# Attention by groups of heads: value products in five stretches of a unit instead of seven

## The chip, the core and the metric

The kernel runs on one core of one Trainium2 chip. The metric is the device time of one execution in microseconds; the time of a kernel is the median of its runs. Engines are called by the names of the profile: PE is TensorE (its matrix products), PEld its weight loads, ACT is ScalarE, DVE is VectorE, POOL is GpSimd, SP is SyncE, which issues most transfers.

## The reference

One layer over 2048 tokens of width 448, in float32: a gate mixes an attention branch A and a token-mixing and MLP branch B.

```python
def _A_ref(x, wq, wk, wv, wo):            # 16 heads of 28, one shared key and value head
    q = (x @ wq).reshape(B, S, H, Dh).transpose(0, 2, 1, 3)
    k = x @ wk
    v = x @ wv
    p = _softmax(einsum("bhqd,bkd->bhqk", q, k) * (Dh ** -0.5), axis=-1)
    o = einsum("bhqk,bkd->bhqd", p, v)
    return o.transpose(0, 2, 1, 3).reshape(B, S, H * Dh) @ wo

g = _sigmoid((x * gate_w).sum(-1, keepdims=True))
out = g * _A_ref(x, ...) + (1 - g) * _B_ref(x, ...)
```

`_B_ref` is a layer norm, a product with `w1`, a GELU, a shift of four channel groups by one or two tokens, a product with `w2`, and an MLP (`w3`, GELU, `w4`) with residuals. It and the projections to queries, keys and values are the first 403 us of the kernel and are not touched.

## The kernel before

The attention is the last part. Its work is cut into `NU` = 16 **units**: a block of 512 queries (four of them) by a group of four heads (four of them). In a unit, each of the `NT` = 16 key tiles `kt` of 128 keys is met by each of the four heads `j`. The position `at = 4 * kt + j`, 0 to 63, is called a slot. A slot has

- a score product on TensorE (L858): keys of the tile against 512 queries of the head, into a PSUM bank of 128 x 512 float32,
- its exponential on ScalarE (L860), out of the bank into a probability tile `p` in SBUF; there are `PB` such tiles.

Value products (`pv_group`, L827) take the four probability tiles of one key tile: four products, one for each head, that sit side by side in four column strips of TensorE's array (`tile_position`) and add into one bank, `pv`, of the unit. Each appears as two records in the profile, so one key tile has 8 records.

Score banks come from a ring. It has seven, and a bank is used again in the order in which it was given back:

```python
banks = [mm_tile("bank_0"), mm_tile("bank_1"), misc_tile("bank_2")]
banks += [ps3.tile([P, 512], F32, name=f"bank_{i}") for i in range(3, 7)]
def bank(name):
    ps = banks.pop(0)
    banks.append(ps)
    return ps
```

A score can be written only when the exponential that last read its bank is over. Two other kinds of work take banks from the same ring:

- `max_part` (L210, L211), four times in a unit at the slots `M_AT`: a small product of 128 x 256 and a VectorE maximum of it, for the next unit's softmax.
- output products (`wo_job`: L769, L771, L773), four jobs in a unit, each of three products of 128 x 448 into one bank, then a VectorE operation (L781) that adds the result to the output tile. They belong to the unit before. `pump()` runs one product at each slot of `WO_AT`; a job keeps its bank out of the ring from its first product to its third.

In the first unit the jobs are the rest of the MLP (`w4_job`, slots `W4_AT`), and the last unit has its own list, `WO_LAST`, and no maxima.

The order on each engine is the order in which the program issues the instructions (a manual schedule); each engine runs its own in that order and waits on semaphores. The loop runs through 16 x 16 + 1 key tiles. After the four slots of a key tile, `VISITS` says whether a **stretch** of value products follows, and for which key tiles: `{2: (0, 2)}` means after the scores of key tile 2 the value products of key tiles 0 and 1. An entry that begins below zero takes the last key tiles of the unit before.

When a unit's value products are over, VectorE copies the sums out of `pv` (`sums_begin`, L735). Slot 12 takes the reciprocals of the row sums (`recip`), by way of three transfers (`rt`, `rd`, `rb`); slot 27 does the normalization (`norm`: L753 on VectorE, L756 and L757 on GpSimd), which the output products read.

Of the kernel before, what the change touches and what calls it, by code (L numbers as in the profile page):

```python
# [28 lines left out]
SCALE = DH ** -0.5  # L29
EPS = 1e-5  # L30
SHIFTS = (-1, 1, -2, 2)
PB = 22
MK = 64
LIMIT = 1e12

# [6 lines left out]
def gated_mix_kernel(  # L42
# [653 lines left out]
    with tc.tile_pool(name="s3", bufs=1, reuse_waits="tile") as s3, \  # L696
# [14 lines left out]
        def q_fetch(u):  # L711
            if u < NU:
                q_load(u, s3.tile([P, 512], F32, tag="qr", bufs=1, name=f"qr_{u}"))
# [78 lines left out]
        def w4_job(t):  # L792
            n = NT - 4 + t
            tok = slice(t * P, (t + 1) * P)
            gh, gl = last_g
            held = banks.pop(0)
            ps = held[:, 0:D]
            nc.tensor.matmul(ps, gh[:, tok], w4h[-1][:, 1, :], start=True, stop=False)
            yield
            nc.tensor.matmul(ps, gh[:, tok], w4l[-1][:, 1, :], start=False, stop=False)  # L800
            yield
            nc.tensor.matmul(ps, gl[:, tok], w4h[-1][:, 1, :], start=False, stop=True)
            banks.append(held)
            nc.vector.scalar_tensor_tensor(x1[:, n, :], ps, gi[:, n:n + 1], x1[:, n, :], op0=ALU.mult, op1=ALU.add)
# [4 lines left out]
        def pump():  # L809
            while current[0] or jobs:  # L810
                if not current[0]:
                    current[0] = jobs.pop(0)
                if next(current[0], True) is None:
                    return
                current[0] = None
                return
# [12 lines left out]
            if kt == NT - 1 and u < NU - 1:  # L829
                sums.append(sums_begin(u, pv_of.pop(u)))  # L830

        WO_AT = (33, 36, 37, 40, 43, 44, 48, 50, 52, 53, 54, 55)
        M_AT = (5, 11, 17, 22)
        M_FIRST = (20, 29, 36, 40)
        W4_AT = (22, 29, 36, 37, 38, 41, 49, 50, 51, 54, 58, 61)
        WO_LAST = (36, 37, 38, 49, 50, 51)
        VISITS = {0: (-2, 0), 2: (0, 2), 4: (2, 4), 6: (4, 6), 8: (6, 8), 11: (8, 11), 14: (11, 14)}

        for k in range(NU * NT + 1):
            u, kt = divmod(k, NT)  # L840
            if k < NU * NT:
                if kt == 8 and 0 < u < NU - 1:
                    q_rows(u + 1)
                if kt == 13 and u + 2 < NU:
                    q_begin(u + 2)
                    q_fetch(u + 3)
                if kt == WO_AT[0] // 4 and u > 0:
                    for t in range(4):
                        jobs.append(wo_job(u - 1, t))
                if k == 0:  # L850
                    for t in range(4):
                        jobs.append(w4_job(t))
                pump_at = W4_AT if u == 0 else WO_AT if u < NU - 1 else WO_LAST
                p_of[k] = []
                for j in range(4):
                    n, at = 4 * k + j, 4 * kt + j
                    ps = bank(f"s_{n}")
                    nc.tensor.matmul(ps, kS[0:98, kt * P:(kt + 1) * P], q_of[u][0:98, j, :], start=True, stop=True)  # L858
                    p = s3.tile([P, 512], F32, tag="p", bufs=PB, name=f"p_{n}")
                    nc.scalar.activation(p, ps, AF.Exp, scale=SCALE)  # L860
# [13 lines left out]
            if k == NU * NT:  # L874
                while current[0] or jobs:
                    pump()
            lo, hi = VISITS.get(kt, (0, 0))
            for kk in range(u * NT + lo, u * NT + hi):
# [96 lines left out]
        with tc.If(again > 0, label="redo"):  # L975
            for b in range(NB):
                for g in range(NG):
# [7 lines left out]
                    for kt in range(NT):  # L985
                        for j in range(4):
                            ps = bank(f"s2_{u}_{kt}_{j}")
                            nc.tensor.matmul(ps, kS[0:98, kt * P:(kt + 1) * P], q_of[u][0:98, j, :],
                                             start=True, stop=True)
                            p = s3.tile([P, 512], F32, tag="p", bufs=PB, name=f"p2_{u}_{kt}_{j}")  # L990
                            nc.scalar.activation(p, ps, AF.Exp, scale=SCALE)
# [57 lines left out]
```

## Time and profile before

| | us |
|---|---|
| median of 3 runs | 962.56 (960.89 to 963.39) |
| profiled execution, first to last instruction | 960.5 |
| first score product starts at | 402.8 |
| TensorE busy | 950.6 (99%) |
| ScalarE busy | 648.1 (67%) |
| VectorE busy | 286.4 (30%) |
| mean granted TensorE clock | 0.998 |

In rows of a timeline the columns are the start, the length, the engine, the line, the operation, what it writes and reads, its shape and the count of merged instructions; in square brackets stands the idle time of the engine before it and what ended that. The chain in order of time has a start, a length, the engine, the tile, the line and the count. A row of groups ends with busy time, mean nanoseconds of one, and the idle time before with its releaser. A row of windows has the window, its length, the busy time and count of PE, PEld, DVE, ACT and POOL, the granted clock, the share of the transfer engines and GB/s.

### The profile page before, as it was taken

What the parts mean: (1) busy time and instruction counts of PE and PEld (TensorE: products, weight loads), DVE (VectorE), ACT (ScalarE), POOL (GpSimd) and SP (SyncE); (2) the same over time, 40 slices, a digit from 0 to 9 for tenths busy, and PEclk for the clock granted to TensorE, in tenths of its full rate; (3) what the DMA queues carried; (4) which work ended last, traced back from release to release, by engine and by line L of the source; (5) the groups of instructions that cost most, each with busy time, mean ns of one, the idle gap of its engine ahead of it and who ended that gap; (6) DMA issues with size and microseconds to landing.
All of it is one profiled execution on the core that took longest, in us unless ns stands there. A gap on an engine that the chain in (4) does not pass through costs nothing.

```text
span 960.5 us, 13540 instructions
## 1 busy us (share of the span) xinstructions
PE 950.6 (99%) x5203; PEld 633.0 (66%) x5203; DVE 286.4 (30%) x573; ACT 648.1 (67%) x1266; POOL 112.8 (12%) x136
## 2 busy tenths in 40 slices
PE   9999999999999999999999999999999999999997
PEld 6788888888888888754555555555555555545554
DVE  4664254533432421221222212222122222212112
ACT  5442444322322222499999999999999999999994
POOL 3243400200001420040000000000000000000000
PEclk9999999999999999999999999999999999999999
DMA  9812452111300300021011021011111101210101
GB/s 308 276 42 61 139 164 83 41 53 29 83 1 1 83 1 10 23 56 46 19 48 42 22 78 52 17 36 51 44 59 40 47 18 40 75 49 12 37 13 42
DMA packets 44439, 56.22 MB, mean 59 GB/s; under 512 B 9536, under 2 KB 27664, under 8 KB 44368
## 3 DMA queue, kind: packets, MB, share of 16 engines
q1 hardware_dynamic: 41344, 49.82, 17.7%
q10 hardware_dynamic: 3024, 5.47, 1.6%
q8 instruction: 42, 0.69, 0.3%
q14 instruction: 29, 0.24, 0.1%
HBM read 32.19 MB, written 11.67 MB: 46 GB/s over the span
## 4 chain that ended last, share of the span: by engine, by line
PE 96%; DMA 3%; DVE 0%; SPq 0%; issue 0%
PE bank L858 27%; PE pv L827 24%; PE acc L635 5%; PE acc L637 5%; PE acc L636 5%; PE g L135 4%; PE g L134 4%; PE g L136 4%; DMA w2raw<-in_w_dram 1%; PE hs L421 1%; PE hs L420 1%; PE hs L422 1%; PE bank L773 1%; PE bank L771 1%; PE bank L769 1%; PE g L137 1%
## 5 line engine op out<-in xcount | busy, mean ns | idle before, releaser
L860 ACT ACTIVATE p<-bank 128x512 f32<-128x512 f32 x1024 | 511.4, 642 | 34.3 <-PE bank L858 31.4
L858 PE MATMUL bank<-qs,kS 98*128 98x512 f32 x1024 | 306.0, 408 | 0.0
L858 PEld LDWEIGHTS bank<-qs,kS 98*128 98x128 f32 x1024 | 184.3, 188 | 134.0 <-issue 93.1
L827 PE MATMUL pv<-p,vext 128*32 128x512 f32 x2048 | 243.1, 598 | 0.0
L625 ACT ACTIVATE gh<-g 128x512 fp32r<-128x512 f32 x55 | 32.9, 598 | 182.5 <-PE g L138 182.5
L827 PEld LDWEIGHTS pv<-p,vext 128*32 128x32 f32 x2048 | 58.6, 109 | 116.3 <-issue 108.9
L627 DVE TENSOR_TENSOR gl<-gf,gh 128x512 fp32r<-128x512 f32 x55 | 38.3, 697 | 161.9 <-ACT gf L626 157.6
L635 PE MATMUL acc<-w4h,gh 128*128 128x448 f32 x220 | 79.9, 363 | 0.0
L637 PE MATMUL acc<-w4h,gl 128*128 128x448 f32 x220 | 79.9, 363 | 0.0
L636 PE MATMUL acc<-w4l,gh 128*128 128x448 f32 x220 | 79.7, 362 | 0.0
L781 DVE SCALAR_TENSOR_TENSOR ot<-bank,gg,ot 128x448 f32<-128x448 f32 x44 | 30.0, 684 | 143.3 <-ACT p L860 95.7
L135 PE MATMUL g<-al,w3h 128*128 128x512 f32 x168 | 65.6, 391 | 0.0
L134 PE MATMUL g<-ah,w3h 128*128 128x512 f32 x168 | 65.6, 391 | 0.0
L136 PE MATMUL g<-ah,w3l 128*128 128x512 f32 x168 | 65.6, 391 | 0.0
L756 POOL CAST onh<-on 128x512 fp32r<-128x512 f32 x15 | 9.1, 609 | 472.4 <-DVE on L753 472.4
L211 DVE TENSOR_REDUCE mr<-bank 128x4 f32<-128x256 f32 x60 | 25.6, 427 | 105.5 <-PE bank L210 104.4
L636 PEld LDWEIGHTS acc<-w4l,gh 128*128 128x128 f32 x220 | 41.3, 188 | 4.2
L635 PEld LDWEIGHTS acc<-w4h,gh 128*128 128x128 f32 x220 | 41.3, 188 | 4.1
L637 PEld LDWEIGHTS acc<-w4h,gl 128*128 128x128 f32 x220 | 41.3, 188 | 3.0
L735 DVE COPY o<-pv 128x512 f32<-128x512 f32 x15 | 10.4, 691 | 99.4 <-PE pv L827 99.4
L136 PEld LDWEIGHTS g<-ah,w3l 128*128 128x128 f32 x168 | 31.5, 188 | 6.8
L135 PEld LDWEIGHTS g<-al,w3h 128*128 128x128 f32 x168 | 31.5, 188 | 5.6
(195 smaller groups left out, 971.4 us busy)
## 6 DMA issues: line engine op xcount, KB each, us to landing
qs<-qh SPq DMA_DIRECT2D x32, 224.0 KB
qd<-qf ACTq DMA_DIRECT2D x16, 256.0 KB
rb<-rd SPq DMA_DIRECT2D x15, 256.0 KB
x<-in_x_dram SPq DMA_DIRECT2D x4, 896.0 KB
xd<-xt SPq DMA_DIRECT2D x16, 224.0 KB
w34raw<-in_w_dram SPq DMA_DIRECT2D x7, 512.0 KB
qr<-qd SPq DMA_DIRECT2D x16, 224.0 KB
qs<-ql SPq DMA_DIRECT2D x16, 224.0 KB
```

Of the source, the lines that this page charges most:

```text
L134: nc.tensor.matmul(ps, wh[:, c, :], ah[:, c, :], start=(c == 0), stop=False)
L135: nc.tensor.matmul(ps, wh[:, c, :], al[:, c, :], start=False, stop=False)
L136: nc.tensor.matmul(ps, wl[:, c, :], ah[:, c, :], start=False, stop=False)
L625: nc.scalar.activation(gh, ps, AF.Gelu_apprx_tanh)
L627: nc.vector.tensor_sub(gl, gf, f32(gh))
L635: nc.tensor.matmul(ps, gh[:, tok], w4h[i][:, k, :], start=(f == 0), stop=False)
L636: nc.tensor.matmul(ps, gh[:, tok], w4l[i][:, k, :], start=False, stop=False)
L637: nc.tensor.matmul(ps, gl[:, tok], w4h[i][:, k, :], start=False, stop=(f == stop))
L781: nc.vector.scalar_tensor_tensor(ot_of[n], ps, gg[:, n:n + 1], before, op0=ALU.mult, op1=ALU.add)
L827: nc.tensor.matmul(pv[32 * j:32 * j + 32, :], vext[:, kt, :], ps[j], start=(kt == 0), stop=(kt == NT - 1), tile_position=(0, 32 * j))
L858: nc.tensor.matmul(ps, kS[0:98, kt * P:(kt + 1) * P], q_of[u][0:98, j, :], start=True, stop=True)
L860: nc.scalar.activation(p, ps, AF.Exp, scale=SCALE)
```

## The change

Three lists and one number are changed; no instruction is added or removed.

- `VISITS`: five stretches in a unit instead of seven. Before, five took two key tiles (16 records) and two took three (24 records). After, four take three key tiles (24 records) and one, after key tile 13, takes four (32 records). The first of a unit finishes the unit before, with three key tiles instead of two.
- `WO_AT`: the twelve output products of a unit lie at other slots, from 33 to 61 instead of 33 to 55. `W4_AT` and `WO_LAST` stay.
- `PB`: 28 probability tiles instead of 22.

```diff
-PB = 22
+PB = 28
...
-        WO_AT = (33, 36, 37, 40, 43, 44, 48, 50, 52, 53, 54, 55)
+        WO_AT = (33, 35, 38, 41, 44, 47, 50, 52, 54, 57, 59, 61)
         M_AT = (5, 11, 17, 22)
         M_FIRST = (20, 29, 36, 40)
         W4_AT = (22, 29, 36, 37, 38, 41, 49, 50, 51, 54, 58, 61)
         WO_LAST = (36, 37, 38, 49, 50, 51)
-        VISITS = {0: (-2, 0), 2: (0, 2), 4: (2, 4), 6: (4, 6), 8: (6, 8), 11: (8, 11), 14: (11, 14)}
+        VISITS = {0: (-3, 0), 3: (0, 3), 6: (3, 6), 9: (6, 9), 13: (9, 13)}
```

## The prediction

> **What bounds the kernel now.** I read the page first: the engines' busy time, the chain that ended last, and the costliest groups.
>
> ```profile
> span 960.5 us, 13540 instructions
> PE 950.6 (99%) x5203; PEld 633.0 (66%) x5203; DVE 286.4 (30%) x573; ACT 648.1 (67%) x1266; POOL 112.8 (12%) x136
> ...
> PE 96%; DMA 3%; DVE 0%; SPq 0%; issue 0%
> ...
> L860 ACT ACTIVATE p<-bank 128x512 f32<-128x512 f32 x1024 | 511.4, 642 | 34.3 <-PE bank L858 31.4
> L858 PE MATMUL bank<-qs,kS 98*128 98x512 f32 x1024 | 306.0, 408 | 0.0
> ```
>
> TensorE looks like the only limit: it is never idle and carries 96% of the chain. But the change lies wholly in attention (the sixteen units from about 403 us on), and there the exponentials (L860) take 511.4 us and idle only 34.3, nearly all of it waiting for a score bank. So two engines are nearly level, and the page's 67% for ScalarE hides it. How they meet is read next, from the chain in order of time: one pair of scores and value products, then the same long stretch of value products in one unit, in the next, and eight units after that.
>
> ```profile
> 571.15 2.06 PE bank L858 x8
> 573.21 1.85 PE pv L827 x16
> ...
> 595.54 2.71 PE pv L827 x24
> ...
> 629.55 2.71 PE pv L827 x24
> ...
> 901.79 2.71 PE pv L827 x24
> ```
>
> One unit takes (901.79 - 629.55) / 8 = 34.03 us. A value product leaves two records, so a key tile (four products) has 8, and 8 records cost 2.71 - 1.85 = 0.86 us.
>
> The timeline of ScalarE shows what the exponentials make of it. The rows come from overlapping windows, so a start can be taken between two rows that end together.
>
> ```profile
> 566.64 4.06 ACT L860 ACTIVATE p<-bank 128x512 f32<-128x512 f32 x8
> 571.68 26.24 ACT L860 ACTIVATE p<-bank 128x512 f32<-128x512 f32 x52 [0.98 <-PE bank L858]
> ...
> 594.34 3.58 ACT L860 ACTIVATE p<-bank 128x512 f32<-128x512 f32 x7
> ...
> 596.72 1.20 ACT L860 ACTIVATE p<-bank 128x512 f32<-128x512 f32 x2
> 598.78 1.09 ACT L860 ACTIVATE p<-bank 128x512 f32<-128x512 f32 x2 [0.85 <-PE bank L858]
> ```
>
> Between the starts 594.34 and 596.72 lie five exponentials: 0.476 us each, start to start, when nothing is missing. Sixty-four of them need 30.46 us. A unit's other 34.03 - 30.46 = 3.57 us are starts that came late. The eight exponentials from 566.64 should have led on at 570.45; the next one came at 571.68, so the 24-record stretch in between cost ScalarE 1.22 us. The seven from 594.34 should have led on at 597.67; the next came at 598.78, so the other 24-record stretch cost 1.10 us. The five 16-record stretches share the rest, 3.57 - 2.32 = 1.25 us, 0.25 each. **A 24-record stretch costs ScalarE over four times what a 16-record one does.** The reason is the ring of seven score banks: during a stretch no score is made, and ScalarE lives on what is in the ring. The 595 us stretch shows that TensorE cannot lay up more first:
>
> ```profile
> 594.57 0.97 PE L858 MATMUL bank<-qs,kS 98*128 98x512 f32 x3
> 595.04 0.19 PEld L858 LDWEIGHTS bank<-qs,kS 98*128 98x128 f32 x1 [0.28 <-ACT p L860]
> 595.47 2.78 PE L827 MATMUL pv<-p,vext 128*32 128x512 f32 x24
> ```
>
> The last score waited for an exponential to free its bank, so the ring was full, and still ScalarE ran dry 1.10 us before the stretch was over. (Five exponentials were then unstarted: counted in steps of 0.476 from 594.34, those of 595.29 to 597.20; the first after the stretch came 3.74 us behind the last score, which is PE's stretch and the way through it.)
>
> **The change, part by part.**
>
> *Two stretches fewer.* By the rows below, ending together, three scores take 572.12 - 571.43 = 0.69 us, 0.23 each.
>
> ```profile
> 571.43 1.79 PE L858 MATMUL bank<-qs,kS 98*128 98x512 f32 x7
> ...
> 572.12 1.09 PE L858 MATMUL bank<-qs,kS 98*128 98x512 f32 x4
> ...
> 575.56 0.28 PE L210 MATMUL bank<-khd,qh 112*128 112x256 f32 x1
> 575.68 1.56 PE L858 MATMUL bank<-qs,kS 98*128 98x512 f32 x6
> ...
> 598.52 0.37 PE L769 MATMUL bank<-woh,onh 128*128 128x448 f32 x1
> 598.73 0.63 PE L858 MATMUL bank<-qs,kS 98*128 98x512 f32 x2
> ```
>
> The pair in the chain takes 2.06 + 1.85 = 3.91 us, of which 8 x 0.23 + 2 x 0.86 = 3.56 is work: going into and out of a stretch costs 0.35 us. Two fewer in each of 16 units take 32 x 0.35 = 11.2 us from TensorE. The count of matrix products stays.
>
> *Longer stretches.* A unit has now five of 24 and 16 records; after the change it has four of 24 (after score slots 3, 15, 27, 39 of the unit) and one of 32 (after 55). Is the ring full before each? From the rows above an output product takes 0.21 and a maximum 0.12 us. TensorE's work from one stretch's end to the next one's end, against ScalarE's time with 1.10 us lost (1.96 = 1.10 + 0.86 for 32 records):
> - slots 56 to 3: 12 scores 2.76, stretch 2.58 + 0.35, three output products 0.63: 6.32, against 5.71 + 1.10 = 6.81
> - 4 to 15, and 16 to 27: two maxima 0.24 in place of those: 5.93, against 6.81
> - 28 to 39: 6.32, against 6.81
> - 40 to 55: 16 scores 3.68, 3.44 + 0.35, six output products 1.26: 8.73, against 7.62 + 1.96 = 9.58
>
> TensorE has 0.5 to 0.9 us to spare each time, so it reaches the full ring and waits there; its 33.3 us no longer set the unit. What sets it is a loop through both engines: stretch, first score, exponentials, a bank freed, last score. Its length is 30.46 + 4 x 1.10 + 1.96 = 36.82 us, if every stretch costs what the fuller of the two measured ones did. With 1.22 instead, it is 37.42. I take the middle, 37.12: the ring will be full, which speaks for 1.10, but the last six output products end one slot before the 32-record stretch, and the first exponential after a gap starts its successor a little later. Per unit that is 37.12 - 34.03 = 3.09 us, over 16 units 49.4 us (44.6 to 54.2). That holds the gain of 11.2 us already, since the loop, not TensorE's work, is counted.
>
> One condition: in the measured full case one of the last seven ring uses was an output tile, which leaves six banks to scores. In the new order that is so everywhere too: slot 61 before 3, 11 before 15, 22 before 27, 38 before 39, 54 before 55, all within seven uses. Only the last unit, which has no maxima, has stretches with all seven, and these cost one exponential less, 1.10 - 0.48 = 0.62 us; there the old 16-record stretches were cheaper as well, so I count that unit like the others.
>
> *Output products spread.* They still fall into the same unit, and start at slot 33. What they read is ready earlier:
>
> ```profile
> 586.10 0.61 POOL L756 CAST onh<-on 128x512 fp32r<-128x512 f32 x1 [32.06 <-DVE on L753]
> 586.79 1.28 POOL L757 TENSOR_TENSOR onl<-on,onh 128x512 fp32r<-128x512 f32 x1
> ...
> 588.73 0.37 PE L769 MATMUL bank<-woh,onh 128*128 128x448 f32 x1
> ```
>
> The high part is there at 586.71, 2.0 us before its first reader. The row chain behind it (copy of the sums, three transfers on SP's queue, reciprocal, product) begins after the stretch that follows slot 3, now 0.86 us longer, and has the whole longer unit to run in; slots 22 to 33 also hold a longer stretch than now. So no new wait; if the cover went, each microsecond of lateness would hold TensorE for as much, 15 times. Copy of the sums and the next unit's first value product (same bank) lie twelve slots apart instead of eight. SP's and POOL's orders are otherwise unmoved. Cost 0.
>
> *28 probability tiles.* The most that the new order keeps is kt 9 to 13, 20 tiles, before the last stretch. No row names ScalarE waiting for a value product to free a tile: 31.4 of its 34.3 us were waits for scores. Worth 0, either way.
>
> *Ends.* After the last exponential one more key tile remains, at most 0.86 us; it lies within the range.
>
> Sum: span 960.5 + 49.4 = 1009.9 us. The profiled execution lies 2.1 us under the median of the runs, so the median goes to 962.6 + 49.4 = 1012.0.
>
> **Rivals.**
>
> *TensorE stays the limit, faster.* Then only the 11.2 us count: 962.6 - 11.2 = 951.4. For it: PE at 99%, 96% of the chain. It decides if a full ring covers a 24-record stretch, that is, if ScalarE loses under (33.3 - 30.46) / 5 = 0.57 us at each; the two measured lost 1.10 and 1.22. The Trainium skill, TensorEngine Tiling (Array Packing), Key Properties, says that changing the tiling mode drains TensorE; the 0.35 us agrees with a drain, and by that rule alone fewer switches are simply faster. Chance 0.03; that gain and loss cancel within 0.3% (2.9 us, about what a measurement here can tell from no change) 0.01.
>
> *A fuller ring.* If every stretch began with seven score banks, it would lose 0.62 (24) or 1.48 (32): 30.46 + 3.96 = 34.42 us a unit, 0.39 x 16 = 6.2 us more, 968.8. Against it: the ring slots above. Chance 0.05.
>
> *The clock falls.* With TensorE waiting at every stretch, its granted clock may drop. These windows are the first unit and the end:
>
> ```profile
> 402.80:436.70 33.90, 33.87 (x196) 17.91 (x196) 7.91 (x17) 31.16 (x63) 11.24 (x6) 1.00 0.23 63
> ...
> 935.00:960.50 25.50, 18.39 (x122) 10.18 (x114) 6.70 (x21) 13.00 (x31) 1.15 (x1) 0.93 0.11 40
> ```
>
> At 0.93 the 3.74 us between last score and first exponential grow by 0.28, five times in 16 units: 22 us more, 1034. The first unit speaks against it: three scores in a row waited for banks there, 0.20 to 0.30 us each, at a clock of 1.00.
>
> ```profile
> 404.88 0.19 PEld L858 LDWEIGHTS bank<-qs,kS 98*128 98x128 f32 x1 [0.20 <-ACT p L860]
> ...
> 405.37 0.19 PEld L858 LDWEIGHTS bank<-qs,kS 98*128 98x128 f32 x1 [0.30 <-ACT p L860]
> ...
> 405.86 0.19 PEld L858 LDWEIGHTS bank<-qs,kS 98*128 98x128 f32 x1 [0.30 <-ACT p L860]
> ```
>
> The Trainium skill, TensorE: Matmul & The Clock Gate, "A second HAM failure mode: psum-queue depth-cycling", describes such a kernel, whose short idles between groups throttled it; this trace does not agree so far. Chance 0.04.
>
> **How the numbers follow.** The loop has 0.87. Its bounds, 44.6 and 54.2 us, give 1007 to 1017; the waits at a bank repeat several times before each stretch, which I have only seen three in a row, and the last unit is roughly counted, so I widen it to 1003 to 1022 for eight in ten. Slower by over 0.3%: 0.87 + 0.05 + 0.04 = 0.96; faster 0.03; same 0.01.
>
> **What would show it.** One more row of before, from the waits (total, times, longest):
>
> ```profile
> PEld bank L858 <- ACT p L860: 9.0, 44, 0.3
> ```
>
> Right: units 37 us apart; on ScalarE five gaps a unit, four of about 0.85 us of idle and one of 1.7, and nearly none else; weight loads of L858 waiting for ScalarE's p in every segment, three or four in a row, hundreds in all instead of 44; granted clock 1.00. Wrong: units of 33.3 us with TensorE free of bank waits; or gaps of 0.4 us; or TensorE held at an output product by POOL or VectorE.

## The result, and the profile after

The changed kernel takes 1011.8 us (median of 4 runs, 1010.7 to 1013.8) against 961.7 of the kernel before (4 runs, the first table's three and one more beside them): a ratio of 1.052, 95% interval 1.051 to 1.054. That is slower by 50 us. The forecast was 1012.0, range 1003 to 1022. The profiled execution spans 1008.9 us, 48.4 more than before. The page counts 65 instructions fewer in all, but on each of the five engines as many as before.

The page of the changed kernel, engines and costliest groups (line, engine, operation, out<-in, count | busy, mean ns of one | idle before, releaser):

```profile
span 1008.9 us, 13475 instructions
PE 999.5 (99%) x5203; PEld 632.4 (63%) x5203; DVE 286.6 (28%) x573; ACT 647.2 (64%) x1266; POOL 112.8 (11%) x136
PE 98%; DMA 0%; ACT 0%; DVE 0%; issue 0%
L860 ACT ACTIVATE p<-bank 128x512 f32<-128x512 f32 x1024 | 510.3, 655 | 84.4 <-PE bank L858 84.4
L858 PE MATMUL bank<-qs,kS 98*128 98x512 f32 x1024 | 350.9, 428 | 0.5
L827 PE MATMUL pv<-p,vext 128*32 128x512 f32 x2048 | 236.3, 596 | 0.0
```

Read alone, this page says that TensorE is still 99% busy. It isn't: the score products show 350.9 us busy, 44.9 more than before, for the same 1024 products. The records overlap: before, 1024 of 0.408 us each are 418 us and cover only 306.0. Where a bank has to be waited for, scores and their weight loads start 0.49 us apart (607.06 - 606.57 in the last rows of this section) instead of 0.23, and by the trace the score's record there lasts 0.50 instead of 0.39. Either way one record reaches the next, so the wait doesn't show as idle time of TensorE. Two other places tell it. ScalarE's idle time before the exponentials went from 34.3 to 84.4 us, all of it put down to scores. And the waits of the changed kernel (total, times, longest) have the score's weight loads waiting for exponentials 274 times instead of 44:

```profile
ACT p L860 <- PE bank L858: 84.4, 80, 2.7
PEld bank L858 <- ACT p L860: 75.0, 274, 0.3
```

Each of the two engines waits for the other: TensorE ahead of a stretch, because the ring is full, ScalarE during it, because the ring runs empty. ScalarE's timeline over one unit of the changed kernel shows the five gaps:

```profile
597.61 5.99 ACT L860 ACTIVATE p<-bank 128x512 f32<-128x512 f32 x12 [0.85 <-PE bank L858]
604.45 5.99 ACT L860 ACTIVATE p<-bank 128x512 f32<-128x512 f32 x12 [0.86 <-PE bank L858]
611.29 7.95 ACT L860 ACTIVATE p<-bank 128x512 f32<-128x512 f32 x16 [0.85 <-PE bank L858]
621.06 5.99 ACT L860 ACTIVATE p<-bank 128x512 f32<-128x512 f32 x12 [1.83 <-PE bank L858]
627.83 5.99 ACT L860 ACTIVATE p<-bank 128x512 f32<-128x512 f32 x12 [0.78 <-PE bank L858]
634.66 2.55 ACT L860 ACTIVATE p<-bank 128x512 f32<-128x512 f32 x5 [0.84 <-PE bank L858]
```

Twelve exponentials at 0.476 us are 5.71 us, but the next block starts 6.84 us later: 1.13 us late. Block by block the starts come late by 1.13, 1.13, 2.15 (after the 32-record stretch: 9.77 less 16 x 0.476), 1.06 and 1.12 us; in all 6.59, and with 30.46 that is the unit's 634.66 - 597.61 = 37.05 us. Just before one of these stretches the timeline of TensorE has the full ring, with two of the weight loads' waits for a bank:

```profile
606.57 0.19 PEld L858 LDWEIGHTS bank<-qs,kS 98*128 98x128 f32 x1 [0.30 <-ACT p L860]
607.06 0.19 PEld L858 LDWEIGHTS bank<-qs,kS 98*128 98x128 f32 x1 [0.30 <-ACT p L860]
...
607.98 2.78 PE L827 MATMUL pv<-p,vext 128*32 128x512 f32 x24
```

### The profile page after: what moved, and what is told of

It reads as the page before. It is cut to its first block, busy times and chain, and to the rows that moved or that the text cites. A ratio compares the mean times of both kernels' runs of the same rounds, so it can differ in the third digit from the quotient of the medians.

```text
span 1008.9 us, 13475 instructions
## 1 busy us (share of the span) xinstructions
PE 999.5 (99%) x5203; PEld 632.4 (63%) x5203; DVE 286.6 (28%) x573; ACT 647.2 (64%) x1266; POOL 112.8 (11%) x136
## 4 chain that ended last, share of the span: by engine, by line
PE 98%; DMA 0%; ACT 0%; DVE 0%; issue 0%
PE bank L858 31%; PE pv L827 23%; PE acc L635 4%; PE acc L637 4%; PE acc L636 4%; PE g L134 4%; PE g L135 4%; PE g L136 4%; PE bank L769 2%; PE hs L421 1%; PE hs L420 1%; PE hs L422 1%; PE bank L773 1%; PE bank L771 1%; PE g L137 1%; PE g L138 1%
## 5 line engine op out<-in xcount | busy, mean ns | idle before, releaser
L860 ACT ACTIVATE p<-bank 128x512 f32<-128x512 f32 x1024 | 510.3, 655 | 84.4 <-PE bank L858 84.4
L858 PE MATMUL bank<-qs,kS 98*128 98x512 f32 x1024 | 350.9, 428 | 0.5
L827 PE MATMUL pv<-p,vext 128*32 128x512 f32 x2048 | 236.3, 596 | 0.0
L134 PEld LDWEIGHTS g<-ah,w3h 128*128 128x128 f32 x168 | 31.5, 188 | 5.5
```

Source lines behind the costliest of these rows:

```text
L134: nc.tensor.matmul(ps, wh[:, c, :], ah[:, c, :], start=(c == 0), stop=False)
L827: nc.tensor.matmul(pv[32 * j:32 * j + 32, :], vext[:, kt, :], ps[j], start=(kt == 0), stop=(kt == NT - 1), tile_position=(0, 32 * j))
```

## The experiments

The theory: during a stretch ScalarE lives on the scores laid up in the ring. What a stretch costs is the time from the last score ahead of it to the first exponential behind it, less the exponentials that the ring can hold; a slot of the ring that an output product or a maximum takes near the end holds one exponential less. The rivals: the length of a stretch costs by itself on TensorE; value products wait for the last exponentials, or 22 tiles are too few; the slots of the output products made the difference. The kernels below ran beside the kernel before. Those with one time are compared with one run of before on the same chip, 962.9 us (first four) or with its median there, 961.2; the runs of before beside the later ones lie between 960.4 and 963.5. Differences to the changed kernel are to the 1011.8 us above, which was not run beside them. A gap by the starts is the time from the start of one exponential to the start of the next, of which 0.48 us is no loss.

### The stretches alone

```diff
-        VISITS = {0: (-2, 0), 2: (0, 2), ..., 14: (11, 14)}
+        VISITS = {0: (-3, 0), 3: (0, 3), 6: (3, 6), 9: (6, 9), 13: (9, 13)}
```

> Before, with the five stretches alone: the old slots of the output products and 22 probability tiles. Ring theory (a stretch costs ScalarE what the seven score banks can't cover): about 37.2 us a unit and 1013 us in all, 51 over before; gaps in the exponentials' starts of about 1.57 us at three 24-record stretches, 1.1 at the one after slot 3 (no output product close ahead of it now) and about 3.1 at the 32-record one, where six output products crowd ahead of slot 55. Rival (the spread output products or the 28 tiles make the kernel slow, the stretches save their 11 us): about 951 us. Rival (22 tiles are too few for five stretches): ScalarE waits for value products by name, and the time lies well over 1015.

Measured: 1013.5 us, 50.6 over before. The five stretches alone do all of it; the output products' slots and the 28 tiles are not needed for the loss. In the waits of this kernel, with its 22 tiles, ScalarE's exponentials wait for scores only:

```profile
ACT p L860 <- PE bank L858: 87.9, 80, 2.7
PEld bank L858 <- ACT p L860: 86.5, 332, 0.3
```

So 22 tiles are enough for five stretches. The units take 37.2 us, and the gaps fall where the slots said: by the starts, 1.07 us (expected 1.1) after slot 3, 1.57 at the next three, 3.17 (3.1) after slot 55. The last one has two causes: by the trace three exponentials are unstarted when its stretch begins, instead of four at the three before, and the output product of slot 55 itself lies between the last score and the stretch.

### The output products alone

```diff
-        WO_AT = (33, 36, 37, 40, 43, 44, 48, 50, 52, 53, 54, 55)
+        WO_AT = (33, 35, 38, 41, 44, 47, 50, 52, 54, 57, 59, 61)
```

> Before, with the new slots of the output products alone: seven stretches, 22 tiles. The prediction gave the spreading a cost of 0. Ring theory, walked through slot by slot with the measured durations: the jobs now hold a bank across the stretches after slots 47 and 59 (50 and 57 to 61), so six banks are left ahead of them; gaps of about 1.8 and 2.3 us instead of 1.58 and 1.69, TensorE waiting four times a unit, 35.3 us a unit, about 979 us in all, 17 over before. Rival (only stretch lengths count, the prediction's 0): 962.

Measured: 979.8 us, 16.9 over before, with the stretches of before. ScalarE's timeline over the end of a unit:

```profile
597.51 5.99 ACT L860 ACTIVATE p<-bank 128x512 f32<-128x512 f32 x12 [0.29 <-PE bank L858]
604.55 5.99 ACT L860 ACTIVATE p<-bank 128x512 f32<-128x512 f32 x12 [1.05 <-PE bank L858]
612.01 8.14 ACT L860 ACTIVATE p<-bank 128x512 f32<-128x512 f32 x16 [1.48 <-PE bank L858]
```

The two 24-record stretches now leave ScalarE idle for 1.05 and 1.48 us, where the kernel before shows 0.85 and 0.98. The stretches are the same, but two things differ, and only one is the ring. Ahead of the first, after slot 47, the ring holds as much as before: by both traces four exponentials are unstarted when the stretch begins, and the expectation was wrong to see a bank held across it. What is new is the third product of a job (L773), which slot 47 puts between the last score and the stretch:

```profile
600.60 0.19 PEld L858 LDWEIGHTS bank<-qs,kS 98*128 98x128 f32 x1 [0.30 <-ACT p L860]
600.94 0.37 PE L773 MATMUL bank<-woh,onl 128*128 128x448 f32 x1
601.24 2.78 PE L827 MATMUL pv<-p,vext 128*32 128x512 f32 x24
```

From the load of that score to the first exponential behind the stretch it is 604.55 - 600.60 = 3.95 us, against 598.78 - 595.04 = 3.74 before: 0.21 us more, which is one output product, beside 0.20 more of idle time. The 16-record stretch after slot 35 pays the same (0.29 us idle, against 0.10 in the trace of before). After slot 59 both come together: a product at slot 59 itself, and a job that keeps its bank from slot 57 to 61, so that three exponentials are laid up instead of four. So the slots of other work cost in two ways: they take banks out of the ring, and they lengthen the way from the last score to the next one.

### The same stretches, with the ring left to scores

```diff
-        WO_AT = (33, 35, 38, 41, 44, 47, 50, 52, 54, 57, 59, 61)
-        M_AT = (5, 11, 17, 22)
+        WO_AT = (40, 41, 42, 43, 44, 45, 46, 47, 48, 56, 57, 58)
+        M_AT = (16, 17, 18, 19)
```

This is the changed kernel with other slots for the same jobs.

> The changed kernel with the same five stretches, but output products right behind stretches (slots 40 to 48 and 56 to 58) and the maxima at 16 to 19, so that none lies in the last seven ring uses ahead of a stretch and no bank is held there. Ring theory: the ring then holds one more score, so a 24-record stretch opens a gap of about 1.08 us in the starts instead of 1.57 and the 32-record one about 2.15 instead of 2.6: about 34.7 us a unit and 978 us in all, 33 less than the changed kernel though its stretches and their work are the same. Rivals (the length of a stretch on TensorE costs by itself; value products wait for the last exponentials of their key tile): 37 us a unit, about 1011, no change.

Measured: 978.1 us, 33.7 under the changed kernel with every stretch as long as there, 15.1 over the kernel before. ScalarE's timeline over a unit:

```profile
593.84 5.99 ACT L860 ACTIVATE p<-bank 128x512 f32<-128x512 f32 x12 [0.36 <-PE bank L858]
600.19 7.94 ACT L860 ACTIVATE p<-bank 128x512 f32<-128x512 f32 x16 [0.36 <-PE bank L858]
609.61 5.99 ACT L860 ACTIVATE p<-bank 128x512 f32<-128x512 f32 x12 [1.48 <-PE bank L858]
615.95 5.99 ACT L860 ACTIVATE p<-bank 128x512 f32<-128x512 f32 x12 [0.35 <-PE bank L858]
622.29 3.04 ACT L860 ACTIVATE p<-bank 128x512 f32<-128x512 f32 x6 [0.35 <-PE bank L858]
```

The idle time fell by 0.49 us at the 24-record stretches after slots 15, 27 and 39, which is one exponential: by the trace five were unstarted when these stretches began, instead of four. After slot 3 it fell by 0.43, after slot 55 by 0.35. This rules out that a 24-record stretch costs by its length alone, and that value products wait for their last exponentials: neither has changed here.

### A smaller ring

```diff
-        banks += [ps3.tile([P, 512], F32, name=f"bank_{i}") for i in range(3, 7)]
+        banks += [ps3.tile([P, 512], F32, name=f"bank_{i}") for i in range(3, 7)]; spare = banks.pop()
...
+        assert not sums and not norms; banks.append(spare)
```

First in the kernel before:

> Before, with six score banks instead of seven (the seventh is given back only for the tail). Ring theory: the seven stretches stay as long, but each opens with one exponential (0.48 us) less laid up: gaps of about 2.08 us at both 24-record stretches and 1.0 to 1.2 at most 16-record ones, 36.7 us a unit, about 1002 us in all, 40 over before. Rival (stretch length and its entry and exit on TensorE set the time): near 962, since the stretches are those of before.

Measured: 1000.3 us, 37.3 over before. By the starts, both 24-record stretches open gaps of 2.05 us and the 16-record ones mostly 1.04 to 1.14; a unit takes 36.55. Then in the changed kernel:

> The changed kernel with six score banks instead of seven. Ring theory: gaps of about 2.08 us at the 24-record stretches instead of 1.57, and about 3.0 at the 32-record one; 39.2 us a unit, about 1045 us in all, 33 over the changed kernel. Rival (the gaps come from the stretches' own time on TensorE): about 1012, as with seven banks.

Measured: 1045.5 us, 33.8 over the changed kernel. ScalarE's timeline there, around the 32-record stretch:

```profile
616.76 5.99 ACT L860 ACTIVATE p<-bank 128x512 f32<-128x512 f32 x12 [1.33 <-PE bank L858]
624.09 7.95 ACT L860 ACTIVATE p<-bank 128x512 f32<-128x512 f32 x16 [1.34 <-PE bank L858]
634.24 5.99 ACT L860 ACTIVATE p<-bank 128x512 f32<-128x512 f32 x12 [2.21 <-PE bank L858]
```

One bank less, one exponential less: 0.48 to 0.49 us more idle at three of the four 24-record stretches (0.85 to 1.34), while the stretches are the same. The one after slot 3 lost 0.31 more and the 32-record one 0.38 (1.83 to 2.21). The same price is seen in both directions, with a bank taken away here and a ring slot given back above.

### Shorter stretches

```diff
-        VISITS = {0: (-2, 0), 2: (0, 2), ..., 14: (11, 14)}
+        VISITS = {i: (i - 1, i) for i in range(NT)}
```

> Before, with a stretch after every key tile (sixteen of 8 records), nothing else changed. TensorE is the bound then: nine stretches more at 0.34 us each way in and out are 3.0 us a unit, 36.9 to 37.0 us a unit and about 1007 us in all; ScalarE loses 0.2 to 0.6 us at each of sixteen stretches and TensorE waits for no bank. The ring theory and the price of a stretch agree here. Rival (shorter stretches are always better, ScalarE alone sets the time): 31 to 33 us a unit, under 950.

Measured: 1009.7 us, 48.5 over before. Of the 44 waits of a score for an exponential one is left, 0.8 us; TensorE is the bound. The chain of this kernel, one pair of four scores and one key tile's value products:

```profile
600.48 1.00 PE pv L827 x8
601.48 1.13 PE bank L858 x4
```

Of the 2.13 us, 0.86 + 4 x 0.23 = 1.78 is work and 0.35 the way in and out. Nine stretches more in 16 units are 48.5 / 144 = 0.34 us each. So the price behind the 11 us on TensorE holds; in the changed kernel it falls on an engine that no longer sets the time.

```diff
-        VISITS = {0: (-2, 0), 2: (0, 2), ..., 14: (11, 14)}
+        VISITS = {i: (i - 2, i) for i in range(0, NT, 2)}
```

> Before, with eight stretches of 16 records instead of five of 16 and two of 24. TensorE is the bound: one stretch more, 0.34 us a unit, less 0.1 us of waits for a bank that go: 34.2 to 34.3 us a unit, about 965 us, 3 over before. Rival (the two 24-record stretches cost the time of before through ScalarE): without them faster than before, by 1.7 us a unit or 25 in all.

Measured: 965.7 us, ratio 1.0046 (1.0028 to 1.0064). Without any 24-record stretch the kernel is still not faster: in the kernel before those stretches' gaps lie under TensorE's work.

### Fewer stretches within what the ring can cover

```diff
-        VISITS = {0: (-2, 0), 2: (0, 2), ..., 14: (11, 14)}
-        WO_AT = (33, 36, 37, 40, 43, 44, 48, 50, 52, 53, 54, 55)
-        M_AT = (5, 11, 17, 22)
+        VISITS = {0: (-2, 0), 2: (0, 2), 4: (2, 4), 7: (4, 7), 10: (7, 10), 14: (10, 14)}
+        WO_AT = (33, 34, 35, 44, 45, 46, 47, 48, 49, 50, 51, 52)
+        M_AT = (20, 21, 22, 23)
...
```

The jobs of the first unit (`M_FIRST`, `W4_AT`) moved behind stretches too; the last unit keeps the seven stretches of before (`V_LAST`).

> Six stretches (three of 24 or 32 records: after slots 31, 43 and 59) with all output products and maxima right behind stretches, so that none stands in the last seven ring uses ahead of a long one; the last unit keeps the seven of before; jobs of the first unit moved likewise. Ring theory: gaps of about 1.05 us at the two 24-record stretches and 2.15 at the 32-record one, in all 30.5 + 3.2 us, just under TensorE's own 33.7: TensorE stays the bound and saves one stretch's entry and exit, 0.34 us a unit, 5 us in all, about 957. Rival (a ring full of scores is worth nothing, as each 24-record stretch costs 1.1 and the 32-record one 2.0): 30.5 + 4.3 = 34.8 us a unit, 973.

Measured: 968.4 us, ratio 1.007 (1.0057 to 1.0083); the expected 957 was missed by 11. In the units but for the first the gaps agree, 1.10, 1.08 and 2.25 us by the starts; a unit takes 33.87 us, 0.16 less than before where 0.34 was expected. The first unit took 44.1 us. Its waits:

```profile
DVE x L804 <- POOL x L605: 8.1, 1, 8.1
PEld bank L858 <- DVE x L804: 8.0, 1, 8.0
PE bank L858 <- DVE x L804: 7.5, 1, 7.5
```

Here the ring was held by something else. The first job of the MLP's rest ended at slot 22, but VectorE could only empty its bank when GpSimd had weighted `x1` (L605), which comes behind the split of `wo`. In the kernel before that job is spread to slot 36 and finds the weights ready. So a job behind a stretch is right only if its bank can be emptied at once. The windows of this kernel around and after that wait (length, PE, PEld, DVE, ACT, POOL busy, granted clock, share of the transfer engines, GB/s) have a lower clock besides:

```profile
412.00:422.00 10.00, 2.46 (x12) 1.81 (x11) 1.79 (x4) 3.85 (x8) 8.14 (x4) 0.74 0.02 6
422.00:436.00 14.00, 14.00 (x75) 6.61 (x75) 1.56 (x5) 9.01 (x18) 3.02 (x3) 0.82 0.01 1
```

With the first unit left as it was:

```diff
-            lo, hi = VISITS.get(kt, (0, 0))
+            lo, hi = (V_LAST if u in (0, NU - 1) else VISITS).get(kt, (0, 0))
```

`M_FIRST` and `W4_AT` are those of before again.

> The six stretches with jobs right behind them in units 1 to 14 only; the first and the last unit as before. The kernel with six stretches in all units lost 10 us in its first unit, where an output tile of the MLP's rest was asked for before GpSimd had its weights applied, and ran its other units in 33.87 us instead of 34.03. Ring theory: that first unit comes back to 34.0 us and the rest stays: 0.16 us in 14 units, 2 to 4 us under before, about 958. Rival (the six stretches themselves cost, the first unit's loss comes with them): 965 or more.

Measured: 959.1 us against 961.6 (10 and 15 runs), ratio 0.9976 (0.9965 to 0.9987). It beats both kernels, by the little that was left: 14 units at 0.16 us are 2.2, measured 2.5 (1.2 to 3.4 by the interval). TensorE still waits for banks, 105 times instead of 44, and ScalarE for scores, so the kernel sits on the balance, which fits that half of the 0.34 us was not gained:

```profile
PEld bank L858 <- ACT p L860: 19.3, 105, 0.3
ACT p L860 <- PE bank L858: 35.9, 48, 2.7
```

## Why the prediction was right

Point by point:

- *The bound.* The loop through ring and stretch sets the changed units: shown, by taking a bank away (0.48 us at most 24-record stretches) and by giving a ring slot back (0.49), with the stretches unchanged. The waits came as said, three or four before each stretch: by the trace at slots 1 to 3, 12 to 15, 24 to 27, 37 to 39 and 49 to 52.
- *Its length.* Predicted 37.12 us a unit between bounds of 36.82 and 37.42, measured 37.05. Two errors cancel in part: a 24-record stretch cost 1.12 us rather than the 1.16 taken (1.06 the one after slot 3, where the last output product lies seven uses back), and the 32-record stretch 2.15 rather than 2.02. The thought behind the higher middle value, that the ring is not quite full ahead of the last stretch, fits that one alone: there the waits end at slot 52, three slots early. How much of the 0.13 us comes from that is not shown. That the median was met to 0.2 us is luck: the rise was 50 us rather than 49.4, on a median before that came out 0.8 lower than the one taken. (The rows as printed give 1.23 and 1.11 us for the two old losses, not 1.22 and 1.10; it moves the unit by 0.05.)
- *The 11 us on TensorE.* The price of a stretch, 0.35 us, was confirmed at 0.34 with sixteen of them. It is not gained, as said. The Trainium skill, TensorEngine Tiling (Array Packing), Key Properties, has changes of tiling mode drain TensorE; these runs agree that going in and out costs, 0.34 us, though none shows the drain itself, and they show that fewer switches can still make a kernel slower.
- *The output products' slots, cost 0.* In the new order the sum held, 37.2 us a unit with the stretches alone and 37.05 with the new slots, but by luck. By the starts, the gap after slot 3 grew from 1.07 to 1.50 us, since a product at slot 61 now lies within the ring's last seven uses, and the gap after slot 55 shrank from 3.17 to 2.6, since no product stands at slot 55 any more; the two cancel. The step looked only at what the jobs read. Alone, in the old order, the same slots cost 16.9 us, in part through the ring and in part through products between the last score and a stretch; that side of the step was missing.
- *28 tiles, worth 0.* No row of the waits of a kernel with 22 has an exponential waiting for a value product.
- *First and last unit counted like the others.* The exponentials' starts give 2.8 us more for the first and 3.7 for the last, against 3.0 for each of the rest. The last was said to have stretches that cost 0.62 us; its starts after slots 15 and 27 were 0.59 late.
- *The rivals.* The fuller ring was built in the third experiment: its price for a 24-record stretch, 0.62 us, came out at 0.63, but the 32-record one lost 1.80 rather than 1.48 and the kernel took 978.1 us rather than 968.8. The clock stayed at 1.00 through hundreds of short waits: 0.999 over the whole execution. The Trainium skill, TensorE: Matmul & The Clock Gate, "A second HAM failure mode: psum-queue depth-cycling", tells of a bf16 kernel whose frequent short idles made its clock swing; these traces show no such fall while each wait is about 0.3 us. In the kernel with one wait of 7.5 us it did fall, to 0.74 and then 0.82.

## What to carry to other kernels

Two engines that pass tiles through a ring are level only as long as the maker's breaks are shorter than what the ring holds: price a break as its length, entry to first use, less stock times the taker's pace, and see what other work sits in the ring ahead of it or between the last tile and the break. A grouping that saves the maker's switches makes its breaks longer; do it until the taker, with what it loses, needs as long as the maker and not beyond, which here was one step, worth 0.24% with the other work moved behind the stretches, not two. And where the maker's records run on into one another, a maker at 99% busy may be waiting: compare the busy time of the same instructions between two kernels, or read the weight loads' waits.

## What was not expected of the hardware

In two kernels the granted clock fell in the first unit while TensorE had no idle time there. The windows of the stretches-alone kernel and of the changed kernel, the same work in the same order:

```profile
407.00:412.00 5.00, 5.00 (x27) 1.38 (x27) 0.00 (x0) 3.15 (x7) 0.00 (x0) 0.66 0.92 258
```

```profile
407.00:412.00 5.00, 5.00 (x34) 2.23 (x33) 0.09 (x1) 4.64 (x11) 0.00 (x0) 1.00 0.97 253
```

In the first of them, the stretches alone, the first stretch of 24 records took 4.48 us instead of 2.78, about 1.7 us once in the execution. The changed kernel with six banks shows it too, at 0.69; the other nine kernels, before among them, show 1.00 in this window. Each is one profiled execution, so it isn't shown whether it belongs to these kernels or to chance. What sets it off was not tried and stays open.
